# Where the spatial bias is added, when operands and weight sums are prepared, and which engine squares, in a three-stage kernel

## The chip, the cores and the metric

The program runs on one core of one Trainium2 chip. The metric is device microseconds of one execution, as the median of several runs. TensorE, VectorE, ScalarE, GpSimd and SyncE are called PE, DVE, ACT, POOL and SP, as in the profile; PEld is PE's weight load. SP and POOL issue the DMAs here: SP's queue takes nearly all loads, POOL's takes the stores, the scatters and the accumulating DMAs.

## The reference

Three parts follow one another on 4 batches of 3072 positions with 256 channels:

```python
scores = scale * np.matmul(z, z.transpose(0, 2, 1))
attn = np.maximum(scores, 0.0) ** 2
x = u * np.matmul(attn, v)                                   # attention
out[mask] = gate_w * eom * (relu(x[mask] @ w1[e]) @ w2[e])   # 8 experts, one for each token
u, v = split(relu(x @ w_in))                                 # 512 + 512 channels
v_n = (v - mean) / sqrt(var + 1e-6)
v_s = np.einsum('ts,bsd->btd', w_spatial, v_n) + b_spatial[None, :, None]
out = (u * v_s) @ w_out
```

The change concerns the bias `b_spatial` (one number for each position t), the operands of the einsum, and the squares of the attention.

## The kernel before

Every float32 operand is split into a rounded part `hi` (ACT copies it) and a remainder `lo` (DVE subtracts), and each product is three matmuls (hi by hi, lo by hi, hi by lo).

**Attention** (`attention`) makes 576 steps: 4 batches b, 6 column blocks j, 24 row blocks k. A step makes one 128x512 block of scores on PE, relu (ACT, `r`), the square rounded (ACT, `hi`), the square exact (`a`: ACT where `i % 3 == 1`, else DVE), the remainder (DVE, `lo`), and the product with v of three steps earlier. Beside it generators are pumped: `fore` (routing of the finished tokens, with indirect DMAs from POOL), `back` (loads and splits of the next batch; in the last batch, at j = 2, `w_prep` loads the first expert's weights through POOL's queue) and `slow`. From the second pass on, `slow` holds `first_sums`: 36 rounds, each with two loads of `w_spatial` into `raw4` buffers (three in all), four sums on DVE and four stores of the sums from POOL. A round takes five pumps. The buffers `raw4` serve `w_prep` too.

**Experts** (`moe`) and **produce** follow. `produce` makes u and v_n, writes u to `u_hid` and sums of v_n to `v_ops`.

**Products** (`products`) computes the einsum by a two-level scheme of seven products each (Strassen's in Winograd's form): seven outer products n in the order 1, 6, 7, 2, 5, 3, 4, and in each seven inner ones m in the order 1, 2, 6, 7, 5, 3, 4, each in two column halves tb, each in three steps kp. So there are 294 steps of 24 matmuls, and a group (n, m, tb) is three steps. Four of the outer products (2, 5, 3, 4, here called the finishing ones) give blocks of the output; the others are combined through a DRAM tensor `partial` with three slots X1, U2, U3: 1 writes X1, 6 reads X1 and writes U2, 7 reads U2 and writes U3, 2 reads X1, 5 reads U3 and adds to U2, 3 reads U2, 4 reads U3. Four things feed a step:

- `p_load` and `p_split`: the weights of a step come by SP into `raw` (three buffers, five steps ahead) and are split into `wh` (ACT, L1307) and `wl` (DVE, L1308) two steps ahead of their matmuls.
- `right`: 21 items (m, kk) for each n. It loads blocks of `v_ops` through SP into `ra` (and `rt` for m = 6, four blocks for an item), combines them on DVE (L1051 to L1059) and splits them (L1008 ACT, L1009 DVE). Each `yield` ends a pump; the queue `back` gets three pumps after each step.
- `evacuate`: after the last step of a group it combines the four PSUM banks with `ut` tiles (L1139 to L1149), and in four of the seven m adds the tile `xi` read from `partial` (two buffers; SP loads it in `x_load`, L1117). In a finishing product it then multiplies by `us` (u from `u_hid`, SP), splits the result into `gt` (L1181 ACT, L1184 DVE), and the gated tile goes to `out`, which multiplies by w_out and stores. In products 6 and 7 it stores `xi` to `partial` (L1168, POOL). `evacuate` advances by four pumps of `fore` after each step.
- The bias: it is added to slots of `partial` in DRAM by `add_bias`, an accumulating DMA from POOL that reads `b_spatial` for all 128 partitions and adds it to 768 KB: 8 of them to X1 during product 6, and 8 to U2 and 8 to U3 during product 7.

All engines but POOL run their instructions in the order in which the program issues them; POOL's order is shown below. A DMA whose source or buffer is not ready holds everything behind it in its queue.

Of the kernel before, what the change touches and what calls it, by code (L numbers as in the profile page):

```python
# [27 lines left out]
F32 = mybir.dt.float32  # L28
# [4 lines left out]
ALU = mybir.AluOpType  # L33
AX = mybir.AxisListType

P = 128
# [18 lines left out]
class _Kernel:  # L55
# [142 lines left out]
    def attention(self):  # L198
# [44 lines left out]
        for i, (b, j, k) in enumerate(steps):  # L243
# [25 lines left out]
            a = self.big.tile([P, 512], F32, name="a", bufs=2)  # L269
            if i % 3 == 1:  # L270
                nc.scalar.activation(a, r, AF.Square)  # L271
            else:
                nc.vector.tensor_tensor(a, r, r, op=ALU.mult)  # L273
# [11 lines left out]
            if i < NK:  # L285
                self.pump(self.back)
                self.pump(self.slow)
                self.pump(self.slow)
            elif i % 2 == 0 and (b == B - 1 or j in (1, 3, 4)):
                self.pump(self.slow)  # L290
# [722 lines left out]
    def right(self, n, dst):  # L1013
# [26 lines left out]
        for i, (m, kk) in enumerate(todo):  # L1040
            load(i + 1)
            yield
            if m == 7:
                a = t3.pop(kk)
            elif m == 4:
                a = t4.pop(kk)
            else:
                a = raws.pop(i)
# [33 lines left out]
    def products(self, steps, NR, pw, p_load, p_split, first):  # L1082
# [7 lines left out]
        block = lambda t: t.rearrange("p (d t) -> p d t", d=4)  # L1090
        ready, due, later, st, xin = deque(), deque(), deque(), {}, {}

        def at(m, tb):
            th, p = self.INNER[m]
            return p, (2 * th + tb) * 384
# [9 lines left out]

        def add(dst, src):
            nc.gpsimd.dma_start(dst, src, accum_op=ALU.add)

        def add_bias(src, m, tb, h):
            t = h * 1536 + at(m, tb)[1]  # L1110
            bias = self.bsp[t : t + 384].partition_broadcast(P).unsqueeze(1).to_broadcast([P, 4, 384])
            add(place(src, m, tb), bias)

        def x_load(n, m, tb):
# [4 lines left out]
        def u_load(n, m, tb, t):  # L1119
            b, t0 = target(n, m, tb)  # L1120
            nc.sync.dma_start(block(t), self.uh[b][:, :, t0 : t0 + 384])
            return t

        def evacuate(n, m, tb, acc):
# [6 lines left out]
            if m in (2, 5):  # L1131
                o = utile()
            us = None
            if o is not None and n in self.BLOCK:
                us = u_load(n, m, tb, self.ok.tile([P, 4 * 384], F32, name="us", bufs=1))
            for d in range(4):
# [21 lines left out]
            if n == 5:  # L1158
                add(place(self.U2, m, tb), block(o))
            r = xin.pop((m, tb))  # L1160
# [6 lines left out]
            if n not in self.BLOCK:  # L1167
                nc.gpsimd.dma_start(place(self.WRITES[n], m, tb), block(r))  # L1168
                if n == 6:
                    add_bias(self.X1, m, tb, 0)  # L1170
                else:
                    add_bias(self.U2, m, tb, 0)
                    later.append((self.U3, m, tb, 1))
                return
            for h in range(2):
                tt(wide(r, h), wide(r, h), wide(us, h), op=ALU.mult)
                yield
# [28 lines left out]
        for s, (n, m, tb, kp) in enumerate(steps[:-3]):  # L1206
# [17 lines left out]
            if kp == 2:  # L1224
                self.drain(self.fore)
                due.extend(ready)
                ready.clear()
                while later:
                    add_bias(*later.popleft())
                self.fore.append(evacuate(n, m, tb, acc))  # L1230
            for _ in range(4):
                self.pump(self.fore)
# [6 lines left out]
        x_load(n, m, tb)  # L1239
        us = u_load(n, m, tb, utile())  # L1240
        r, u, g = xin.pop((m, tb)), st["u", tb], []
# [19 lines left out]
        for h in range(2):  # L1261
            tt(wide(r, h), wide(r, h), wide(u, h), op=ALU.subtract)
        out(other[0], 0)
        column(1)
# [132 lines left out]
```

## Time and profile before

| | us |
|---|---|
| median of three runs | 3561.55 (3560.2 to 3566.04) |
| the profiled execution | 3547.28 |
| its span, first to last instruction | 3545.5 |
| PE busy | 3402.7 |
| DVE busy | 2535.8 |
| ACT busy | 1791.7 |
| POOL busy | 747.3 |

Busy time of the PE counts matmuls whatever clock they ran at, so a stretch in which the clock was down looks busier than what it achieved; the number of matmuls in a stretch tells more. The stages of the profiled execution are: attention to about 1130 us, experts to about 1760, produce to about 2070, products to the end.

### The profile page before, as it was taken

The numbers are of one execution on the slowest core, as the hardware profiler recorded it, in microseconds if no ns is written. First come the engines' busy times: TensorE is split into PE (matmuls) and PEld (weight loads), VectorE is DVE, ScalarE is ACT, GpSimd is POOL, SyncE is SP. The second block draws the span as 40 slices with busy tenths as digits, with TensorE's granted clock in tenths as the row PEclk, the third lists the DMA queues.
The fourth block names the chain that finished last, engine by engine and source line by source line (L and its number), as shares of the span: only waits on it lengthen the run. The fifth ranks groups of instructions, "written<-read, shape, count | busy, mean of one in ns | idle before, by whom it ended". The sixth has DMA issues, their size and how long they took to land.

```text
span 3545.5 us, 51148 instructions
## 1 busy us (share of the span) xinstructions
PE 3402.7 (96%) x18448; PEld 3094.1 (87%) x18448; DVE 2535.8 (72%) x4616; ACT 1791.7 (51%) x3110; POOL 747.3 (21%) x1092
## 2 busy tenths in 40 slices
PE   8999999999999999999999999996957999999999
PEld 6888887887787999999988889996957999999999
DVE  7777777788787788777588865664625776776766
ACT  8888878878776333333254533332312333343433
POOL 3111111121222566665423210000010000100000
PEclk9999999999999999999999999998978999999999
DMA  7232231233332777777477874979999577885754
GB/s 258 80 101 64 81 101 55 80 105 96 110 121 100 253 265 255 266 269 248 166 277 284 319 277 152 292 186 282 223 187 253 183 268 222 237 272 178 262 199 153
DMA packets 277480, 689.31 MB, mean 194 GB/s; under 512 B 30128, under 2 KB 126144, under 8 KB 277216
## 3 DMA queue, kind: packets, MB, share of 16 engines
q1 hardware_dynamic: 181536, 401.90, 33.9%
q0 software_dynamic: 95680, 284.06, 25.8%
q8 instruction: 145, 2.38, 0.3%
q14 instruction: 119, 0.97, 0.1%
HBM read 440.26 MB, written 264.45 MB: 199 GB/s over the span
## 4 chain that ended last, share of the span: by engine, by line
PE 72%; DMA 10%; issue 9%; POOL 3%; DVE 3%; ACT 2%; SPq 0%; POOLq 0%; DVEq 0%; ACTq 0%
PE bank L1195 10%; PE bank L1196 9%; PE bank L1194 9%; PE bank L226 7%; PE bank L227 7%; PE bank L225 7%; DMA ra<-v_ops 4%; PE bank L263 4%; PE bank L264 3%; PE bank L735 2%; PE bank L671 2%; PE bank L673 2%; PE bank L736 2%; PE bank L672 2%; PE bank L737 2%
## 5 line engine op out<-in xcount | busy, mean ns | idle before, releaser
L275 DVE TENSOR_TENSOR lo<-a,hi 128x512 fp32r<-128x512 f32 x576 | 398.2, 692 | 184.0 <-ACT a L271 93.9
L1194 PE MATMUL bank<-wh,R 128*128 128x384 f32 x1288 | 435.5, 338 | 49.1 <-ACT wh L1307 44.9
L1195 PE MATMUL bank<-wl,R 128*128 128x384 f32 x1288 | 436.2, 339 | 20.9 <-DVE wl L1308 20.9
L226 PE MATMUL bank<-lo,G 128*128 128x512 f32 x1152 | 451.9, 392 | 2.2 <-DVE lo L275 2.2
L225 PE MATMUL bank<-hi,G 128*128 128x512 f32 x1152 | 450.3, 391 | 0.0
L227 PE MATMUL bank<-hi,G 128*128 128x512 f32 x1152 | 449.7, 390 | 0.0
L1196 PE MATMUL bank<-wh,R 128*128 128x384 f32 x1288 | 434.9, 338 | 0.0
L1308 DVE TENSOR_TENSOR wl<-raw,wh 128x768 fp32r<-128x768 f32 x294 | 280.6, 955 | 197.2 <-ACT wh L1307 195.3
L266 ACT ACTIVATE r<-bank 128x512 f32<-128x512 f32 x576 | 342.5, 595 | 153.9 <-PE bank L264 144.2
L1307 ACT ACTIVATE wh<-raw 128x768 fp32r<-128x768 f32 x294 | 247.2, 841 | 337.7 <-PE bank L1196 193.9
L1194 PE MATMUL bank<-wh,K 128*128 128x384 f32 x1064 | 358.7, 337 | 19.2 <-ACT wh L1307 19.2
L1195 PE MATMUL bank<-wl,K 128*128 128x384 f32 x1064 | 359.1, 337 | 15.9 <-DVE wl L1308 15.9
L268 ACT ACTIVATE hi<-r 128x512 fp32r<-128x512 f32 x576 | 364.9, 633 | 18.3
L1196 PE MATMUL bank<-wh,K 128*128 128x384 f32 x1064 | 357.9, 336 | 0.0
L739 ACT ACTIVATE hh<-bank 128x512 fp32r<-128x512 f32 (+2 forms) x256 | 132.7, 518 | 392.2 <-PE bank L737 349.7
L1194 PEld LDWEIGHTS bank<-wh,R 128*128 128x128 f32 x1288 | 245.4, 191 | 51.7 <-ACT wh L1307 46.7
L273 DVE TENSOR_TENSOR a<-r 128x512 f32<-128x512 f32 x384 | 263.1, 685 | 23.9 <-ACT r L266 23.2
L1195 PEld LDWEIGHTS bank<-wl,R 128*128 128x128 f32 x1288 | 245.0, 190 | 24.2 <-DVE wl L1308 24.2
L226 PEld LDWEIGHTS bank<-lo,G 128*128 128x128 f32 x1152 | 217.1, 188 | 52.9 <-DVE lo L275 7.6
L225 PEld LDWEIGHTS bank<-hi,G 128*128 128x128 f32 x1152 | 217.2, 189 | 46.6 <-ACT hi L268 0.3
L741 DVE SCALAR_TENSOR_TENSOR hlo<-bank,hh 128x512 fp32r<-128x512 f32 (+2 forms) x256 | 150.6, 589 | 149.0 <-ACT hh L739 133.3
L227 PEld LDWEIGHTS bank<-hi,G 128*128 128x128 f32 x1152 | 217.1, 188 | 45.3
(298 smaller groups left out, 8048.9 us busy)
## 6 DMA issues: line engine op xcount, KB each, us to landing
raw<-w_parts SPq DMA_DIRECT2D x240, 384.0 KB
ra<-v_ops SPq DMA_DIRECT2D x147, 512.0 KB
raw<-wsq SPq DMA_DIRECT2D x126, 384.0 KB
v_ops<-vu POOLq DMA_DIRECT2D x84, 512.0 KB
xi<-partial SPq DMA_DIRECT2D x48, 768.0 KB
w_parts<-raw POOLq DMA_DIRECT2D x144, 192.0 KB
u_hid<-vu POOLq DMA_DIRECT2D x48, 512.0 KB
us<-u_hid SPq DMA_DIRECT2D x31, 768.0 KB
```

The costliest lines, as they stand in the source:

```text
L225: nc.tensor.matmul(acc[d], vh[:, c], hi, start=(k == 0), stop=False)
L226: nc.tensor.matmul(acc[d], vh[:, c], lo, start=False, stop=False)
L227: nc.tensor.matmul(acc[d], vl[:, c], hi, start=False, stop=(k == NK - 1))
L266: nc.scalar.activation(r, sb, AF.Relu, scale=1.0 / S)
L268: nc.scalar.activation(hi, r, AF.Square)
L273: nc.vector.tensor_tensor(a, r, r, op=ALU.mult)
L275: nc.vector.tensor_tensor(lo, a, _f(hi), op=ALU.subtract)
L1194: nc.tensor.matmul(ps, vh, wh[:, ws], start=(k == 0), stop=False)
L1195: nc.tensor.matmul(ps, vh, wl[:, ws], start=False, stop=False)
L1196: nc.tensor.matmul(ps, vl, wh[:, ws], start=False, stop=(k == 5))
L1307: nc.scalar.activation(hi, raw, AF.Copy)
L1308: tt(lo, raw, _f(hi), op=ALU.subtract)
```

## The change

Five things are changed. (1) The accumulating bias DMAs are gone. Each finishing product's `evacuate` loads 384 numbers of the bias for all partitions into a tile `bb` (192 KB, SP, right behind `us`) and adds it on DVE with two additions of 128x768, before the multiplication; the last group does the same. (2) `evacuate` is advanced by 3, 3 and 4 pumps in a group's steps instead of 4, 4, 4. (3) `right` yields once more in each item, and twice more at its first item of m = 6. (4) `first_sums` is pumped in other passes of the last batch: at every step of j = 1 and not at all in j = 2. (5) ACT makes a fourth of the squares `a` instead of a third.

```diff
-            if i % 3 == 1:
+            if i % 4 == 1:
                 nc.scalar.activation(a, r, AF.Square)
             else:
                 nc.vector.tensor_tensor(a, r, r, op=ALU.mult)
...
-            elif i % 2 == 0 and (b == B - 1 or j in (1, 3, 4)):
+            elif b == B - 1 and j == 1 or i % 2 == 0 and (j in (1, 3, 4) or b == B - 1 and j in (0, 5)):
                 self.pump(self.slow)
...
             load(i + 1)
             yield
+            yield
+            if m == 6 and kk == 0:
+                yield
+                yield
...
-        def add(dst, src):
-            nc.gpsimd.dma_start(dst, src, accum_op=ALU.add)
-
-        def add_bias(src, m, tb, h):
-            t = h * 1536 + at(m, tb)[1]
-            bias = self.bsp[t : t + 384].partition_broadcast(P).unsqueeze(1).to_broadcast([P, 4, 384])
-            add(place(src, m, tb), bias)
...
             nc.sync.dma_start(block(t), self.uh[b][:, :, t0 : t0 + 384])
-            return t
+            bb = self.ok.tile([P, 384], F32, name="bb", bufs=1)
+            nc.sync.dma_start(bb, self.bsp[t0 : t0 + 384].partition_broadcast(P))
+            return t, bb
...
             if n == 5:
-                add(place(self.U2, m, tb), block(o))
+                nc.gpsimd.dma_start(place(self.U2, m, tb), block(o), accum_op=ALU.add)
...
                 nc.gpsimd.dma_start(place(self.WRITES[n], m, tb), block(r))
-                if n == 6:
-                    add_bias(self.X1, m, tb, 0)
-                else:
-                    add_bias(self.U2, m, tb, 0)
-                    later.append((self.U3, m, tb, 1))
                 return
+            for h in range(2):
+                w = wide(r, h).rearrange("p (d t) -> p d t", d=2)
+                tt(w, w, bb.unsqueeze(1).to_broadcast([P, 2, 384]), op=ALU.add)
+                yield
...
-                while later:
-                    add_bias(*later.popleft())
                 self.fore.append(evacuate(n, m, tb, acc))
-            for _ in range(4):
+            for _ in range(4 if kp == 1 else 3):
                 self.pump(self.fore)
...
             tt(wide(r, h), wide(r, h), wide(u, h), op=ALU.subtract)
+            w = wide(r, h).rearrange("p (d t) -> p d t", d=2)
+            tt(w, w, bb.unsqueeze(1).to_broadcast([P, 2, 384]), op=ALU.add)
```

Lines behind the change have other numbers: L1308 is L1305 in the changed kernel, L1055 is L1059, L1168 is L1166, L1176 is L1173.

The first place is POOL's queue through products 7, 2 and 5. Before, the end of product 7 and the start of what follows (`bsp` is the bias, `xi` the tile that products 6 and 7 store, `os` an output block):

```order
L1107 DMA partial<-bsp 512x1x384 x2
L1168 DMA partial<-xi 512x1x384
L1107 DMA partial<-bsp 512x1x384 x2
L1168 DMA partial<-xi 512x1x384
L1107 DMA partial<-bsp 512x1x384 x2
L1168 DMA partial<-xi 512x1x384
L1107 DMA partial<-bsp 512x1x384
L1080 DMA out<-os 128x384 x16
L1107 DMA partial<-ut 512x1x384 x2
```

In the changed kernel, from product 1 to product 5:

```order
L1154 DMA partial<-ut 512x1x384 x8
L1166 DMA partial<-xi 512x1x384 x16
L1084 DMA out<-os 128x384 x16
L1157 DMA partial<-ut 512x1x384 x2
L1084 DMA out<-os 128x384 x4
```

The 24 accumulating DMAs that stood between the stores of `xi` are gone; the eight of `ut` in product 5 stay.

The second place is DVE at the start of the products. Before, from the last instruction of `produce`:

```order
L939 TENSOR_TENSOR vu_19995<-vu_19995,vu_19987 128x1024
L1308 TENSOR_TENSOR wl<-raw,wh 128x768
L1009 TENSOR_TENSOR K_74<-ra,K_74 128x512
L1009 TENSOR_TENSOR K_75<-ra,K_75 128x512
L1308 TENSOR_TENSOR wl<-raw,wh 128x768
L1009 TENSOR_TENSOR K_76<-ra,K_76 128x512
L1055 TENSOR_TENSOR rt<-rt,ra 128x1024
L1308 TENSOR_TENSOR wl<-raw,wh 128x768
```

In the changed kernel, from the second `wl` behind `produce`:

```order
L1305 TENSOR_TENSOR wl<-raw,wh 128x768
L1009 TENSOR_TENSOR K_81<-ra,K_81 128x512
L1009 TENSOR_TENSOR K_74<-ra,K_74 128x512
L1305 TENSOR_TENSOR wl<-raw,wh 128x768
L1009 TENSOR_TENSOR K_75<-ra,K_75 128x512
L1305 TENSOR_TENSOR wl<-raw,wh 128x768
L1009 TENSOR_TENSOR K_76<-ra,K_76 128x512
L1305 TENSOR_TENSOR wl<-raw,wh 128x768
L1059 TENSOR_TENSOR rt<-rt,ra 128x1024
L1305 TENSOR_TENSOR wl<-raw,wh 128x768
```

The first combination of m = 6 (`rt<-rt,ra`) stood behind two `wl` of the products stage and now stands behind five; in each of the seven products it has moved back by three.

The third place is DVE in a finishing product, a group of m = 3 in product 2. Before, from the evacuation of the banks to the gated tile:

```order
L1149 TENSOR_TENSOR ut<-bank_70,ut 128x384
L1149 TENSOR_TENSOR ut<-bank_71,ut 128x384
L1149 TENSOR_TENSOR ut<-bank_72,ut 128x384
L1149 TENSOR_TENSOR ut<-bank_73,ut 128x384
L1165 TENSOR_TENSOR xi<-xi,ut 128x768 x2
L1308 TENSOR_TENSOR wl<-raw,wh 128x768
L1176 TENSOR_TENSOR xi<-xi,us 128x768 x2
L1009 TENSOR_TENSOR K_77<-ra,K_77 128x512
L1308 TENSOR_TENSOR wl<-raw,wh 128x768
L1184 TENSOR_TENSOR gt<-xi,gt 128x768 x2
```

In the changed kernel, the same group up to the multiplication:

```order
L1147 TENSOR_TENSOR ut<-bank_70,ut 128x384
L1147 TENSOR_TENSOR ut<-bank_71,ut 128x384
L1147 TENSOR_TENSOR ut<-bank_72,ut 128x384
L1147 TENSOR_TENSOR ut<-bank_73,ut 128x384
L1163 TENSOR_TENSOR xi<-xi,ut 128x768
L1305 TENSOR_TENSOR wl<-raw,wh 128x768
L1163 TENSOR_TENSOR xi<-xi,ut 128x768
L1170 TENSOR_TENSOR xi<-xi,bb 128x768 x2
L1305 TENSOR_TENSOR wl<-raw,wh 128x768
L1173 TENSOR_TENSOR xi<-xi,us 128x768 x2
```

The bias stands where the multiplication stood, and the multiplication and all behind it come one `wl` later.

## Rows read from the trace of the kernel before

**Rows 1.** The page's chain that ended last: shares of the span by engine

```profile
PE 72%; DMA 10%; issue 9%; POOL 3%; DVE 3%; ACT 2%; SPq 0%; POOLq 0%; DVEq 0%; ACTq 0%
```

**Rows 2.** Stretches: start:end, length, busy us (instructions) by engine, PE clock, DMA share, GB/s

```profile
2060.00:2080.00 20.00, 12.15 (x67) 11.83 (x66) 7.24 (x10) 2.86 (x6) 1.25 (x2) 0.89 0.85 305
2080.00:2380.00 300.00, 300.00 (x1726) 300.00 (x1725) 195.14 (x274) 104.71 (x156) 12.83 (x15) 1.00 0.70 218
2380.00:2480.00 100.00, 71.61 (x367) 69.20 (x366) 47.53 (x61) 25.37 (x41) 8.54 (x9) 0.85 0.97 268
...
2580.00:2760.00 180.00, 116.26 (x599) 110.88 (x598) 75.84 (x101) 35.89 (x57) 15.55 (x15) 0.83 0.93 221
2760.00:3080.00 320.00, 320.00 (x1848) 320.00 (x1847) 225.53 (x310) 119.21 (x182) 20.54 (x30) 1.00 0.70 224
3080.00:3140.00 60.00, 55.74 (x311) 55.11 (x310) 39.94 (x52) 24.43 (x41) 6.31 (x9) 0.97 0.96 303
3140.00:3500.00 360.00, 360.00 (x2079) 360.00 (x2078) 255.86 (x348) 135.24 (x207) 13.56 (x25) 1.00 0.63 213
...
0.00:1140.00 1140.00, 1118.01 (x5026) 906.59 (x5027) 896.81 (x1884) 932.25 (x1637) 211.98 (x334) 1.00 0.31 104
```

**Rows 3.** The chain in 2550 to 2760 us: start, us, what

```profile
2560.33 14.73 DMA xi<-partial
...
2616.65 17.39 DMA partial<-xi
...
2636.39 17.49 DMA ra<-v_ops
```

**Rows 4.** The same chain by line, shares of its 210 us

```profile
by line: DMA ra<-v_ops 27.7%; DMA partial<-xi 14.7%; issue 11.5%; DMA xi<-partial 9.3%; PE bank L1195 8.8%; PE bank L1196 8.3%; PE bank L1194 8.0%; DVE wl L1308 3.2%; ACT wh L1307 2.0%; SPq L1025 1.4%; POOL partial L1107 1.1%; SPq L1300 1.0
```

**Rows 5.** SP's waits in 2550 to 2730 us: us in total, times, longest

```profile
SPq L1117 <- DMA partial<-xi: 53.5, 3, 23.6
```

**Rows 6.** DMA queues in 2440 to 2700 us: packets, MB, share of 16 engines

```profile
q0 software_dynamic: 9945, 18.94, 51.7%
q1 hardware_dynamic: 15217, 38.34, 41.7%
```

**Rows 7.** The bias DMAs on POOL: count, shortest/median/longest ns, first and last start

```profile
L1107 POOL DMA_DIRECT2D partial<-bsp x24: 1147/1166/1721, 2271.1 to 2707.9; - x24
```

**Rows 8.** DVE in order of time, finishing product 2: start, us, instruction, count [idle <-releaser]

```profile
2850.62 1.94 DVE L1149 TENSOR_TENSOR ut<-bank,ut 128x384 f32<-128x384 f32 x4
2852.48 1.81 DVE L1165 TENSOR_TENSOR xi<-xi,ut 128x768 f32<-128x768 f32 x2
2854.21 0.95 DVE L1308 TENSOR_TENSOR wl<-raw,wh 128x768 fp32r<-128x768 f32 x1
2857.63 1.82 DVE L1176 TENSOR_TENSOR xi<-xi,us 128x768 f32<-128x768 f32 x2 [2.47 <-DMA us<-u_hid]
...
2865.98 2.12 DVE L1149 TENSOR_TENSOR ut<-bank,ut 128x384 f32<-128x384 f32 x4 [0.38 <-PE bank L1196]
```

**Rows 9.** DVE in order of time at the start of the products

```profile
2076.37 1.23 DVE L1055 TENSOR_TENSOR rt<-rt,ra 128x1024 f32<-128x1024 f32 x1 [12.72 <-DMA ra<-v_ops]
2077.51 0.95 DVE L1308 TENSOR_TENSOR wl<-raw,wh 128x768 fp32r<-128x768 f32 x1
```

**Rows 10.** Attention: the stretch with the longest PE gap behind the start

```profile
960.00:980.00 20.00, 14.99 (x61) 11.81 (x60) 12.06 (x33) 11.10 (x23) 3.16 (x5) 0.83 0.31 103
```

**Rows 11.** Waits in 930 to 980 us: us in total, times, longest

```profile
ACT K L183 <- DMA raw<-w: 9.5, 3, 6.5
...
POOL raw L446 <- DMA w_parts<-raw: 4.2, 1, 4.2
```

**Rows 12.** Groups of instructions, the exact squares: busy us, mean ns | idle before

```profile
L273 DVE TENSOR_TENSOR a<-r 128x512 f32<-128x512 f32 x384 | 263.1, 685 | 23.9 <-ACT r L266 23.2
...
L271 ACT ACTIVATE a<-r 128x512 f32<-128x512 f32 x192 | 118.3, 616 | 0.6 <-DVE lo L275 0.6
```

**Rows 13.** Waits over the whole run: the multiplication by u

```profile
DVE xi L1176 <- DMA us<-u_hid: 27.1, 20, 3.2
```

**Rows 14.** DVE in order of time near the end: the second last group's gated tile

```profile
3519.56 1.83 DVE L1184 TENSOR_TENSOR gt<-xi,gt 128x768 fp32r<-128x768 f32 x2
```

More of the change, by code (lines that the diff above doesn't have):

```diff
@@ L1090, in products @@
         block = lambda t: t.rearrange("p (d t) -> p d t", d=4)
-        ready, due, later, st, xin = deque(), deque(), deque(), {}, {}
+        ready, due, st, xin = deque(), deque(), {}, {}
         def at(m, tb):
@@ L1134, in evacuate @@
             if o is not None and n in self.BLOCK:
-                us = u_load(n, m, tb, self.ok.tile([P, 4 * 384], F32, name="us", bufs=1))
+                us, bb = u_load(n, m, tb, self.ok.tile([P, 4 * 384], F32, name="us", bufs=1))
             for d in range(4):
@@ L1239, in products @@
         x_load(n, m, tb)
-        us = u_load(n, m, tb, utile())
+        us, bb = u_load(n, m, tb, utile())
         r, u, g = xin.pop((m, tb)), st["u", tb], []
```

## The prediction

> **What bounds the kernel now.** Read the chain that ended last first: PE holds 72% of it, DMA 10%, DVE 3%, ACT 2% [rows 1]. So the time is PE's work plus places where PE waits, and the waits at the end of which something else than PE comes last are mostly transfers. Next read the stretches [rows 2]. Where PE never stops, in 2760 to 3080 and in 3140 to 3500 us, it does 1848 matmuls in 320 us and 2079 in 360, both 5.775 a us. Measured with that rate, the other stretches of the products lost: 2380 to 2480, 577.5 wanted, 367 done, **36.5 us**; 2580 to 2760, 1039.5 wanted, 599 done, **76.3 us** (more than the 63.7 us in which PE is not busy, since the granted clock was 0.83 to 0.85 there, between the two levels of 1.2 and 2.4 GHz); 3080 to 3140, 346.5 wanted, 311 done, 6.1 us. The stretch 2060 to 2080 mixes two kinds of matmuls; by its busy time it lost 7.9 us. In attention 5026 matmuls in 1140 us are 4.41 a us, and 960 to 980 has 61 of 88 [rows 10], 6.2 us. These five sum to 133 us, and the first two are products 6 and 7, into whose time all the bias DMAs fall: 24 of them, from 2271 to 2708 us [rows 7].
>
> Then ask what PE waits for in the two large holes. In 2550 to 2760 the chain has pieces of xi being loaded, 9.3% of 210 us, of xi being stored, 14.7%, and of operands `ra` arriving, 27.7% [rows 3, 4]. SP waited 53.5 us in three pieces for stores of xi [rows 5]: the load of a further xi needs a buffer that POOL's queue has yet to empty, and in that queue a bias DMA stands ahead of each store. All loads of weights and operands stand behind SP's wait. Meanwhile the transfer engines are full, 0.93 to 0.97, at only 221 to 268 GB/s, while product 2 moves 224 GB/s at a share of 0.70 [rows 2]; POOL's queue took 51.7% of the engines' time for 18.94 MB, SP's 41.7% for 38.34 [rows 6]. A byte of the former cost 2.5 times as much.
>
> **1. The bias DMAs go.** 24 transfers of 768 KB leave, and with them the wait of each store of xi behind one. What remains in products 6 and 7 is loads of weights, operands and xi, and 16 stores, much as in product 2, which replaces the stores by loads of u and runs with PE full [rows 2]. A store of xi then still takes somewhere between the time of its bytes at 224 GB/s, 786 KB, 3.5 us, and the 17.39 us of the jam [rows 3]; I take 6, near the lower end, as nothing stands before it. The load that needs the buffer comes some 12 us (three steps of 24 matmuls) behind the group's end, the store about 6 behind it, so at 6 us nothing waits, and at 17 us SP waits some 11, which five steps of prefetch nearly cover. A burst of operand loads may still delay weights at the end of each product, as in 3080 to 3140 [rows 2], where accumulating DMAs of another kind run. So of 113 us I take 105 as won, with bounds 50 (if the pieces of `ra`, half of the chain's transfer time in the hole [rows 4], stay) and 113.
>
> A check by bytes, without waits: 24 times 786 KB are 18.9 MB, at the 221 GB/s of the hole [rows 2] 85 us. By the Trainium skill, "DMA: Bandwidth & Descriptors", section "Issuing engines are not separate DMA queues", transfers that different engines issue run on the same 16 engines and interleave, so that only the transfers themselves count and not that they stood in POOL's queue. By that page the win would be nearer to the 85, and the forecast 20 us higher; the trace speaks for a dearer byte on that queue [rows 6], and I keep 105.
>
> **2. `right` yields more.** The first combination of m = 6 waits 12.72 us for its load, and the `wl` that PE needs stands right behind it on DVE [rows 9]. It now stands three `wl` later, that is three steps of 24 matmuls, 12.5 us: the wait is almost exactly covered. Of the 7.9 us I take 7 (0 to 8). The same move helps in 3080 to 3140: 3 of 6.1 (0 to 6). Twenty-three more yields make 99 pumps an outer product where 126 are given, so the operands come in time; if not, PE would wait for a split. What is behind a moved item on SP, the loads of `raw`, gets ahead of its four loads, which is the better order.
>
> **3. Sums of `first_sums`.** The stall at 960 is w_prep and the sums sharing three buffers: ACT waits 9.5 us for expert weights, POOL 4.2 for a store of sums before it can load them [rows 11]. With no sums in j = 2 that wait goes: 6 us (0 to 6). j = 1 of the last batch gets 12 more pumps, 4.8 rounds of four sums, about 10 us of DVE in 46; DVE has 897 of 1140 busy in this stage [rows 2], so it fits, at a cost of 0 to 4 us, taken as 1. Behind a late sum on DVE stand the remainders `lo`, which PE wants three steps later.
>
> **4. Squares.** 48 squares leave ACT, 48 x 0.616 = 30 us, and 48 x 0.685 = 33 us come to DVE [rows 12]. ACT was at 82% of the stage and DVE at 79% [rows 2]; they change places, PE keeps its work, and I take 0 (-2 to +3). PE's matmuls are the cover; without it the worst is 33 us.
>
> **5. The bias on DVE.** A 128x768 addition starts 0.87 us before the next one (2852.48 to 2854.21 for two, [rows 8]). There are 64 of them, 55 us. In a finishing group DVE's work is 1.86 for the banks and nine operations of 0.87, 9.7 us, and becomes 11.4; with four splits of `right` some 14; PE's group is 96 matmuls, 16.6 us. It fits. What is delayed: the gated tile comes one `wl` later, and `out`, the next group's evacuation and the splits of weights stand behind it. The bias may wait for its load, which SP issues behind that of u; u itself was waited for in 20 places, 27.1 us in all, 3.2 at the most [rows 13]. In place of that wait the later multiplication has none. I take 0.2 us for each of 31 groups, 6 us (0 to 30).
>
> **6. The end.** The gated tile of the second last group is made by DVE at 3519.56 to 3521.4, just as PE wants it [rows 14]. Two additions stand before it now: 2 us (0 to 4).
>
> Sum: 105 + 7 + 3 + 6 - 1 - 6 - 2 = **112 us** against the profiled execution's 3547.3, which gives 3435. The median of the runs is 14.3 us above that execution; whether those 14 us are part of the holes the trace can't show. I let them stand and predict **3449**.
>
> **Rivals.**
> - *Half of the holes stays.* For it: the pieces of `ra` are the largest part of the chain there [rows 4], and the burst hurts at 3080 too, with no bias. Against it: the full stretches have the same bursts. Only 50 of 113 are won: 3504.
> - *DVE becomes the bound.* By the Trainium skill, "Perfetto Trace Analysis", section "Optimizing Scalar/DVE Operations", work should leave the Vector engine when that is the saturated one; this change brings it 88 us. In this kernel that would be DVE chains of finishing groups longer than PE's 16.6 us, so that all 55 us lie on the path instead of 6: 3498. The trace speaks against it: 9.7 us of work [rows 8].
> - *The load of the bias is late* (slower). It stands behind 768 KB of u on SP. A group has 16.6 - 14 = 2.6 us of room on DVE, and 112 us in 31 groups are 3.6 more: from some 6.2 us of waiting in each group the gain is eaten. At 10 us, the kernel is at 3561 + 31 x 3.8, about 3680. The longest wait for u was 3.2 [rows 13].
> - *It does not do what it says:* the holes come from the traffic of products 6 and 7 alone, and removing the bias only moves the wait. Then steps 2 and 3 balance 5 and 6, and the time is about 3555.
>
> **How the numbers follow.** The forecast has 0.70, half of the holes 0.14, DVE 0.08, no effect 0.05, the late load 0.03. The forecast's own bounds: all 113 us won, all of steps 2 and 3, nothing lost and the 14 us gone as well, 3412; 85 won and 20 lost on DVE, 3483. The first two rivals end at 3504; with some DVE loss beside them, 3512. So the range is **3408 to 3512**. A measurement of this kernel can tell about 0.2%, 7 us, from no change. Faster: 0.70 + 0.14 + 0.08 and half of the fourth, 0.94; same 0.02; slower 0.04.
>
> **What would show it.** In the new profile products 6 and 7 should take as many us a matmul as product 2, with the clock at 1.00 and no wait of SP for stores of xi over a few us; the transfer share there should fall from 0.95 to about 0.8. The m = 6 combination at the start should wait little, and no PE gap should stand at 2070 or 960. DVE should be busy in 2760 to the end for some 8 points more, and PE still full. Wrong would be: holes of tens of us in products 6 and 7 with `ra` at the end of the wait; waits of the bias addition of over 3 us in most groups; or PE waiting for `wl` in finishing groups.

## The result and the profile after

| | median of the runs | lowest to highest | profiled execution | its span |
|---|---|---|---|---|
| before | 3561.45 us (4 runs) | 3560.20 to 3566.04 | 3547.28 us | 3545.5 us |
| after | 3418.72 us (4 runs) | 3417.67 to 3421.45 | 3417.67 us | 3415.8 us |

The changed kernel takes 0.9598 of the time before, 95% interval 0.9582 to 0.9615: 143 us by the medians, 129.7 us by the two profiled spans. Of what is forecast above, 3449 us in 3408 to 3512, the time came out 30 us lower.

The first and the fourth part of the page after: busy time, share of the span and instructions by engine, and the chain that ended last.

```profile
PE 3377.8 (99%) x18448; PEld 3080.5 (90%) x18448; DVE 2622.0 (77%) x4728; ACT 1774.9 (52%) x3062; POOL 717.5 (21%) x1068
...
PE 46%; DVE 1%; issue 0%; DMA 0%; ACT 0%; SPq 0%; ACTq 0%; DVEq 0%
```

DMA held 10% of the chain before [rows 1] and now 0%; the chain after can be followed back to some 1758 us only, which is why its shares sum to 47%, but it takes in all the products. PE is the bound nearly everywhere there. The stretches after answer to [rows 2] and [rows 10]. The columns are the same: start:end, length, busy us (instructions) of PE, PEld, DVE, ACT and POOL, PE's clock, DMA share, GB/s. The products begin some 11 us earlier now, so 2240 to 2720 holds nearly all of products 6 and 7 in both kernels, and after the start of product 2 as well.

```profile
0.00:1140.00 1140.00, 1122.94 (x5063) 912.71 (x5063) 933.42 (x1939) 911.85 (x1594) 211.96 (x335) 1.00 0.32 105
...
960.00:980.00 20.00, 20.00 (x94) 16.35 (x93) 17.57 (x48) 16.43 (x30) 3.24 (x4) 0.99 0.18 55
...
2060.00:2080.00 20.00, 20.00 (x117) 20.00 (x117) 14.43 (x16) 9.26 (x15) 0.00 (x0) 1.00 1.01 380
...
2240.00:2640.00 400.00, 397.98 (x2297) 397.69 (x2296) 284.26 (x390) 145.20 (x215) 12.51 (x18) 1.00 0.72 245
2640.00:2720.00 80.00, 80.00 (x463) 80.00 (x462) 58.07 (x84) 29.77 (x44) 2.17 (x4) 1.00 0.59 192
2720.00:3380.00 660.00, 654.39 (x3762) 652.95 (x3761) 507.61 (x677) 248.83 (x383) 37.70 (x59) 1.00 0.73 238
```

Read each against 5.775 matmuls a us. 2240 to 2640 wants 2310 and did 2297: 2.3 us lost. 2640 to 2720 wants 462 and did 463: nothing. For the kernel before, the same two stretches are:

```profile
2240.00:2640.00 400.00, 347.10 (x1935) 343.07 (x1934) 224.96 (x311) 112.42 (x168) 33.89 (x34) 0.94 0.89 231
2640.00:2720.00 80.00, 42.25 (x199) 39.88 (x200) 29.24 (x39) 16.18 (x27) 7.37 (x7) 0.73 1.01 243
```

There it lost 64.9 and 45.5 us. So 108 of 110 us of the holes are gone. The start gap is gone too. 2720 to 3380, the finishing products, wants 3811.5 and did 3762: 8.6 us lost, the most that is left. In attention 5063 matmuls stand where 5026 stood [rows 2], 37 more; at 4.41 a us that is 8.4 us.

What waits after, in 2060 to 3380 us (for whom and for what: us in total, times, longest). All of PE's waits:

```profile
PE bank L1073 <- DVE ut L1139: 4.6, 3, 2.4
PE bank L1073 <- ACT R L1008: 2.0, 1, 2.0
PE bank L1073 <- DVE ut L1147: 1.0, 1, 1.0
```

Of the waits for a transfer, those of DVE and of ACT in the same stretch, and one of SP's over the whole run:

```profile
DVE xi L1170 <- DMA bb<-bsp: 17.5, 14, 2.5
...
ACT R L1008 <- DMA ra<-v_ops: 8.2, 6, 3.2
ACT K L1008 <- DMA ra<-v_ops: 7.1, 5, 2.3
...
SPq L1113 <- DMA partial<-xi: 7.3, 4, 2.3
```

SP waits 7.3 us for stores of xi in the whole run, where one stretch alone had 53.5 [rows 5]. The first combination of m = 6 waits 2.78 us at the start, where it waited 12.72 [rows 9]. The bias is waited for 14 times, 2.5 us at the most.

### The profile page after: what moved, and what is told of

Same layout as the page of the kernel before. It is cut to its first block, busy times and chain, and to the rows that moved or that the text cites. A ratio compares the mean times of both kernels' runs of the same rounds, so it can differ in the third digit from the quotient of the medians.

```text
span 3415.8 us, 51212 instructions
## 1 busy us (share of the span) xinstructions
PE 3377.8 (99%) x18448; PEld 3080.5 (90%) x18448; DVE 2622.0 (77%) x4728; ACT 1774.9 (52%) x3062; POOL 717.5 (21%) x1068
## 5 line engine op out<-in xcount | busy, mean ns | idle before, releaser
L1305 DVE TENSOR_TENSOR wl<-raw,wh 128x768 fp32r<-128x768 f32 x294 | 280.9, 955 | 212.3 <-ACT wh L1304 211.2
L1191 PE MATMUL bank<-wh,R 128*128 128x384 f32 x1288 | 430.4, 334 | 0.0
L1193 PE MATMUL bank<-wh,R 128*128 128x384 f32 x1288 | 430.2, 334 | 0.0
L273 DVE TENSOR_TENSOR a<-r 128x512 f32<-128x512 f32 x432 | 296.4, 686 | 26.5 <-ACT r L266 26.0
```

The costliest lines, as they stand in the source:

```text
L1191: nc.tensor.matmul(ps, vh, wh[:, ws], start=(k == 0), stop=False)
L1193: nc.tensor.matmul(ps, vl, wh[:, ws], start=False, stop=(k == 5))
L1305: tt(lo, raw, _f(hi), op=ALU.subtract)
```

## The experiments

All ratios are against the kernel before, run on the same chip as the kernel in question; there its median was 3549.6 to 3553.2 us. "Lost" is counted as above, with 5.775 matmuls a us. A few windows lie some us apart between kernels.

### What the bias transfers cost, and of what kind the cost is

**e1_bias_dve**: before with part 1 alone.

```diff
...
-                if n == 6:
-                    add_bias(self.X1, m, tb, 0)
-                else:
-                    add_bias(self.U2, m, tb, 0)
-                    later.append((self.U3, m, tb, 1))
...
+            bb = self.ok.tile([P, 384], F32, name="bb", bufs=1)
+            nc.sync.dma_start(bb, self.bsp[t0 : t0 + 384].partition_broadcast(P))
...
+            for h in range(2):
+                w = wide(r, h).rearrange("p (d t) -> p d t", d=2)
+                tt(w, w, bb.unsqueeze(1).to_broadcast([P, 2, 384]), op=ALU.add)
+                yield
...
```

> The kernel before with the first edit alone: no accumulating bias DMAs, the bias loaded into bb and added by DVE in the finishing products; pumps of evacuate, right, sums and squares as before. Theory Q (the holes of products 6 and 7 come from the bias DMAs): most of the 143 us that the changed kernel gained is here, a median of about 3450 us, and products 6 and 7 without PE gaps over some us. Theory R (the bursts of operand loads carry half of the holes): about 3500.

Measured: 3467.18 us, ratio 0.977 (0.9754 to 0.9787). That lies between the two theories' times. The holes themselves are gone, as the first says: 2281 and 463 matmuls in 2240 to 2640 and 2640 to 2720 us, 5.0 us lost of 110. What is missing to 3450 us is lost in the finishing products, as the next run shows.

**e7_no_bias**: before without the bias transfers and without any addition.

```diff
                 nc.gpsimd.dma_start(place(self.WRITES[n], m, tb), block(r))
-                if n == 6:
-                    add_bias(self.X1, m, tb, 0)
-                else:
-                    add_bias(self.U2, m, tb, 0)
-                    later.append((self.U3, m, tb, 1))
```

> The kernel before without the bias DMAs and with no addition in their place: the bias is left out of the result. Beside e1 it tells what the 64 additions on DVE and the 32 small loads cost. Prediction's sum: 6 us less than e1, with bounds 0 and 30. If DVE is the bound of the finishing products: 30 to 55 us less than e1.

Measured: 3439.78 us, ratio 0.9692 (0.9676 to 0.9708). The transfers cost 3.1%, 109 us. But the additions on DVE, with their loads, cost 27 of these in the order of before, as e1 is that much slower; the forecast of 6 is missed and lies within its bounds of 0 and 30. The finishing products show where. First e7, with the larger part of products 6 and 7, then e1:

```profile
2240.00:2640.00 400.00, 397.14 (x2285) 395.54 (x2285) 278.25 (x381) 142.85 (x218) 11.39 (x16) 1.00 0.73 252
...
2720.00:3380.00 660.00, 655.44 (x3769) 654.41 (x3768) 469.31 (x635) 250.41 (x387) 37.60 (x59) 1.00 0.70 231
```

```profile
2060.00:2080.00 20.00, 12.12 (x61) 11.80 (x61) 7.21 (x9) 4.65 (x9) 0.00 (x0) 0.78 0.84 311
...
2720.00:3380.00 660.00, 641.49 (x3633) 637.30 (x3632) 490.35 (x658) 244.84 (x379) 36.00 (x56) 0.98 0.71 229
```

In the last of these stretches e7 lost 7.4 us, e1 30.9. The start gap (61 matmuls of 115) is in both.

**e8_bias_aside**: before, with the same 24 accumulating transfers into rows of `y_tok` that the products don't read.

```diff
...
-            add(place(src, m, tb), bias)
+            i = self.aside % 16
+            self.aside += 1
+            dst = self.yt[i * 768 : (i + 1) * 768, :].rearrange("(p r) d -> p (r d)", p=P)
+            nc.gpsimd.dma_start(dst.rearrange("p (a t) -> p a t", a=4), bias, accum_op=ALU.add)
```

> The kernel before with the same 24 accumulating bias DMAs, at the same places of POOL's queue and with the same bytes, but added to rows of a DRAM tensor that nothing reads any more (y_tok), so that no load or store of partial depends on them; the bias is left out of the result. Theory W (waiting: loads of xi hold SP's queue because of the order between bias, stores and loads on partial): the holes go almost as in e7, within 30 us of it. Theory T (the transfer engines' time is what is short): the holes stay, 80 us or more above e7, though SP's wait for stores of xi is shorter.

Measured: 3552.35 us, ratio 1.0005 (0.9995 to 1.0014). It did not tell the two theories apart as meant. POOL issued the transfers earlier, from 1793 to 2134 us, in the stage `produce`. That stage still loads from `y_tok` (until 2098 us), so the rows are not free there: on POOL the transfers wait 23.3 us for those loads and 59.6 us for one another, and the stores of `v_ops`, which the products read, stand behind them in the queue. The last of these stores comes at 2173.8 us, where before has it at 2060.4, 113 us later. The hole moved with them:

```profile
2060.00:2200.00 140.00, 87.16 (x391) 73.05 (x390) 73.42 (x141) 40.23 (x77) 29.76 (x42) 0.80 0.97 283
```

The transfer engines are full here too, and products 6 and 7 were full of matmuls (2295 and 447). What it does show: the same transfers cost the same at another place, with no load of xi behind them. Other stores stood behind them there, so it doesn't separate the engines' time from the waits.

**e10_copy_plain** and **e11_copy_accum**: e7 with 24 transfers of 768 KB pinned behind the stores of products 6 and 7. They take the result just stored as their source and write rows that nobody reads. e11 accumulates; e10 has the same lines without `accum_op`.

```diff
...
                 nc.gpsimd.dma_start(place(self.WRITES[n], m, tb), block(r))
+                for _ in range(1 if n == 6 else 2):
+                    i = self.aside % 16
+                    self.aside += 1
+                    dst = self.yt[i * 768 : (i + 1) * 768, :].rearrange("(p r) d -> p (r d)", p=P)
+                    nc.gpsimd.dma_start(dst.rearrange("p (a t) -> p a t", a=4), place(self.WRITES[n], m, tb), accum_op=ALU.add)
```

> Built on the kernel without bias (e7_no_bias: before without the 24 bias transfers and without an addition, 3439.8 us, 0.969 of before; the bias is left out of the output). Behind each store of the subtree products, where the bias transfers stood on GpSimd's queue, it puts a plain copy of 768 KB from the partial result just stored to a buffer that nobody reads any more: 24 copies, one behind each store of product 6 and two behind each of product 7, no accumulation. Theory (an accumulating transfer holds the DMA engines for about 7.4 us, a plain one of the same bytes for 2 to 4.5 us, and this engine time is the damage): the copies add at most 24 x 4.5 = 108 us of engine time to a stretch that has slack for about that, so 3440 to 3475 us, 0.969 to 0.978 of before. Rival (the damage comes of the place in the queue: the store is written, its slot is read back and written again before the next load may follow, whatever the kind): 3510 to 3560 us, 0.99 to 1.0, like e11_copy_accum.

> The same kernel as e10_copy_plain with the one difference that the 24 copies accumulate into the buffer that nobody reads (bias left out of the output). Theory (engine time of accumulating transfers): about 177 us of all DMA engines in products 6 and 7 again, as in the kernel before, so most of the 110 us that leaving the transfers out gave is lost again: 3510 to 3560 us, 0.99 to 1.0 of before, and the software queue's share between 2260 and 2720 us is near 46%. Rival (the reader's wait for the accumulated slot was what cost, not engine time): nobody reads these rows, so 3440 to 3480 us, and alike with e10_copy_plain.

Measured: e10 3451.69 us, 0.9714 (0.9698 to 0.973); e11 3480.86 us, 0.9798 (0.9782 to 0.9814). By the ratios plain copies cost 0.22% over e7, 8 us, with an error about as large, as e7 ran on another chip; by the matmuls below, 16 us. Either is inside the theory's 0 to 35, and the rival falls: the place in the queue alone does not cost 70 us or more. Accumulating copies cost 1.06% over e7, 38 us, and 29 us more than the plain ones, on the same chip. So neither expectation for e11 holds: the kind matters, against the rival, but less than the theory said (3510 us or more; POOL's queue should have held near 46% of the engines' time in 2260 to 2720 us, and held 31.4%). Products 6 and 7 in e10, then in e11:

```profile
2240.00:2640.00 400.00, 387.46 (x2197) 383.24 (x2195) 262.90 (x359) 133.37 (x204) 27.66 (x41) 0.99 0.81 290
2640.00:2720.00 80.00, 79.43 (x456) 78.65 (x456) 57.19 (x80) 30.99 (x47) 2.19 (x4) 1.00 0.59 200
```

```profile
2240.00:2640.00 400.00, 374.44 (x2094) 370.43 (x2094) 250.06 (x344) 127.19 (x192) 35.58 (x38) 0.97 0.86 265
2640.00:2720.00 80.00, 73.64 (x404) 72.16 (x403) 53.00 (x69) 27.49 (x45) 4.35 (x6) 0.96 0.82 261
```

Lost: 20.6 us in e10, 47.4 in e11, 110.4 in before, and 4.3 in e7. SP's waits for the stores of xi grow with them. In 2060 to 2720 us, e10, e11 and before have the following, and e7 has no such wait:

```profile
SPq L1118 <- DMA partial<-xi: 4.1, 2, 3.0
```

```profile
SPq L1118 <- DMA partial<-xi: 33.7, 6, 13.1
```

```profile
SPq L1117 <- DMA partial<-xi: 85.2, 5, 23.6
```

In e10 and e11 no load of xi reads what the 24 transfers write. So the longer waits of e11 come from transfers before the stores in POOL's queue, or from the engines that these hold, and not from slots that are read again. The price of one transfer can be read from POOL's queue on the pages (packets, MB, share of 16 engines over the span). In order: e7, e10, e11, e8, before.

```profile
q0 software_dynamic: 83008, 265.18, 21.6%
```

```profile
q0 software_dynamic: 87616, 284.06, 22.9%
```

```profile
q0 software_dynamic: 95680, 284.06, 24.3%
```

```profile
q0 software_dynamic: 95680, 284.06, 25.2%
```

```profile
q0 software_dynamic: 95680, 284.06, 25.8%
```

Times their spans (3434.3, 3453.6, 3478.2, 3551.8, 3545.5 us) and less e7's 741.8 us, the 24 transfers of the same 18.9 MB held all 16 engines for 49, 103, 153 and 173 us: **2.0 us** for a plain copy, **4.3** for an accumulating one, **6.4 and 7.2** for an accumulating one whose source is the broadcast bias (384 numbers read 512 times). A plain copy is 192 packets, an accumulating one 528. So accumulating adds 2.3 us, and the repeated source 2.1 to 2.9 more.

The packets in the traces say where the last part comes from. Of the 528 packets 512 carry 1536 bytes. These take 140 ns in the median in e11, in e8 and in before alike, but 143, 213 and 237 ns in the mean: 2% of them take over 160 ns in e11, 28% in e8 and 31% in before. The slow ones come with the repeated source, at both of its places; the eight accumulating transfers of product 5, whose source is a tile, have a mean of 143 ns as well (e7). Summed by packets the prices come out a little higher, 4.6, 6.8 and 7.6 us, as the queue's other packets took a little less than in e7.

The waits of xi's loads for these very slots, which e11 has not, were not separated from the source: from e11 to before the time rises by some 70 us, and the engines' time by 70 as well.

### What the yields of `right` do

**e2_right_late**: before with part 3 alone.

```diff
             load(i + 1)
             yield
+            yield
+            if m == 6 and kk == 0:
+                yield
+                yield
```

> The kernel before with the added yields of right alone; the bias DMAs stay. Theory Q: only the gap at the start of the products (8 us) and part of that at 3080 us go, the two large holes stay: about 3550. Theory R: the loads of operands are what ends the waits, so spreading them takes half of the holes away: about 3500.

Measured: 3514.6 us, ratio 0.9896 (0.988 to 0.9913): 35 us by the medians and 37 by the ratio, for three added yields. That lies between the two theories' times.

```profile
2060.00:2080.00 20.00, 20.00 (x117) 20.00 (x116) 12.19 (x15) 9.59 (x17) 0.00 (x0) 1.00 1.01 372
...
2240.00:2640.00 400.00, 340.87 (x1893) 335.54 (x1891) 220.22 (x306) 108.70 (x162) 34.29 (x34) 0.93 0.91 232
2640.00:2720.00 80.00, 61.66 (x291) 58.60 (x292) 41.35 (x55) 23.63 (x38) 6.24 (x6) 0.83 1.02 269
2720.00:3380.00 660.00, 659.98 (x3808) 659.66 (x3807) 478.03 (x641) 257.26 (x397) 37.59 (x59) 1.00 0.72 234
```

The start is full, the finishing products lost 0.6 us (9.6 in before), and the holes stay, some 9 us smaller (2184 matmuls in the two stretches, where before had 2134). So spreading the operands' loads does not close the holes, and the yields gain at places that neither theory named.

**e5_undo_right**: the changed kernel without part 3.

```diff
-            yield
-            if m == 6 and kk == 0:
-                yield
-                yield
```

> The changed kernel without the added yields of right. If the yields only matter beside the bias DMAs (e2 alone gave 35 us), this stays within 15 us of the changed kernel: about 0.964 of before. If the finishing products need them too, because DVE's additions stand before loads of operands that come late, as e1 (27 us above e7) lets one think, it falls back by 30 us or more: about 0.970 or above.

Measured: 3460.48 us, ratio 0.9741 (0.9727 to 0.9756), so the yields are worth 1.4%, 51 us, in the changed kernel: the second of the two expectations. Two of its stretches, and two waits in 2060 to 3380 us, PE's first and ACT's for `ra`:

```profile
2060.00:2080.00 20.00, 12.77 (x58) 12.45 (x58) 12.37 (x13) 6.56 (x12) 0.00 (x0) 0.74 0.91 343
...
2720.00:3380.00 660.00, 632.32 (x3574) 625.44 (x3573) 482.58 (x645) 238.57 (x370) 36.07 (x56) 0.99 0.70 228
```

```profile
PE bank L1187 <- ACT os L1079: 20.9, 9, 3.4
...
ACT R L1008 <- DMA ra<-v_ops: 67.6, 12, 13.1
...
ACT K L1008 <- DMA ra<-v_ops: 48.6, 13, 10.3
```

It lost 41.1 us in the finishing products and 10 at the start. ACT waited 116 us for pieces of `ra`; after, 15.3. One such wait, first SP and then ACT in order of time (start, us, instruction, count, [idle <-releaser]):

```profile
2973.91 0.52 SPq L1113 DMA_DIRECT2D us<-u_hid  x1
2974.49 0.61 SPq L1115 DMA_DIRECT2D bb<-bsp  x1
2975.28 0.52 SPq L1109 DMA_DIRECT2D xi<-partial  x1
2978.87 0.33 SPq L1293 DMA_DIRECT2D raw<-w_parts  x1
2979.24 1.50 SPq L1025 DMA_DIRECT2D ra<-v_ops  x2
```

```profile
2974.86 0.85 ACT L1300 ACTIVATE wh<-raw 128x768 fp32r<-128x768 f32 x1 [2.34 <-issue]
2988.51 0.63 ACT L1008 ACTIVATE R<-ra 128x512 fp32r<-128x512 f32 x1 [12.81 <-DMA ra<-v_ops]
2989.05 0.48 ACT L1079 ACTIVATE os<-bank 128x384 f32<-128x384 f32 x1
2989.42 0.84 ACT L1300 ACTIVATE wh<-raw 128x768 fp32r<-128x768 f32 x1
```

SP issues `us`, `bb`, `xi` and `raw` ahead of the two pieces of `ra`. ACT reaches the copy of `ra` at 2975.7 and stands there until 2988.5. Behind it, in ACT's own order, stand `os`, which empties PE's banks, and `wh`, of which DVE makes the next `wl`. PE stops soon after:

```profile
2995.33 0.44 PE L1187 MATMUL bank<-wh,K 128*128 128x384 f32 x1 [3.39 <-ACT os L1079]
```

**e13_one_yield**: the changed kernel without the two extra yields at m = 6.

```diff
-            if m == 6 and kk == 0:
-                yield
-                yield
```

> The changed kernel without the two extra yields before the first combination of m = 6; the one more yield before every combination stays. Without any of the new yields the changed kernel takes 3460.5 us (0.974), with all 0.960. Theory (the one yield in every step does it: it lengthens the way from each load to the copy on ScalarE that waits for it, and ScalarE's evacuations stand behind that copy): 3415 to 3430 us, 0.960 to 0.964. Rival (it is the first combination of m = 6 alone, four tiles at once, that is late): 3445 to 3465 us, 0.970 to 0.976.

Measured: 3413.93 us, ratio 0.9608 (0.9592 to 0.9624), as the changed kernel. The one yield for each item does the work. The rival falls.

The waits of ACT for `ra` and the loss go together over the runs, though not in one ratio. In 2720 to 3380 us the waits are 76.9 us in e1, 63.4 in e5, 31.9 in e7, 7.1 in e2 and 3.4 in e12 (below); lost are 30.9, 41.1, 7.4, 0.6 and 0.8 us. That the wait on ACT is what stops PE is seen in the chain above; no run changed it alone.

### DVE's additions in the changed order

**e12_after_no_bias**: the changed kernel without loads of the bias and additions; the yields of the pumps stay.

```diff
...
-            for h in range(2):
-                w = wide(r, h).rearrange("p (d t) -> p d t", d=2)
-                tt(w, w, bb.unsqueeze(1).to_broadcast([P, 2, 384]), op=ALU.add)
-                yield
+            yield
+            yield
...
```

> The changed kernel without the bias (neither its loads nor VectorE's additions; the pumps' yields stay, so the order of the rest stays), bias left out of the output. In the order of before, without the yields in the right operands' combinations, the additions and loads cost 27 us (3467.2 with, 3439.8 without). Theory (the additions cost only where ScalarE and VectorE already stand behind a late right operand, and the yields have taken that away): 3405 to 3420 us, 0.957 to 0.961, 0 to 10 us under the changed kernel. Rival (VectorE's time itself costs, 62 additions of 0.95 us and the loads of 24 more transfers): 3385 to 3400 us, 0.951 to 0.955, 20 to 30 us under the changed kernel.

Measured: 3406.35 us, ratio 0.9586 (0.957 to 0.9602); its span is 3408.8 us, 7.0 under that of after.

```profile
2720.00:3380.00 660.00, 659.87 (x3807) 659.55 (x3806) 466.14 (x632) 254.85 (x387) 38.14 (x60) 1.00 0.71 232
```

It lost 0.8 us in the finishing products, after 8.6. So the additions and loads that cost 27 us in e1 cost about 7 here (4 by the ratios, which can't tell it from nothing), and the theory holds.

One more rival is a late bias: in e1 the additions wait for `bb`, and in after less. The waits of DVE in 2060 to 3380 us in e1, then in e6, the changed kernel without part 2 (next section):

```profile
DVE xi L1166 <- DMA bb<-bsp: 64.5, 24, 4.6
```

```profile
DVE xi L1170 <- DMA bb<-bsp: 51.0, 23, 4.3
```

e6 still waits 51.0 us where e1 waits 64.5, and yet it is as fast as the changed kernel; in 2720 to 3380 us it did 3782 matmuls and lost 5.1 us. In the products the two differ by the yields of `right` alone. So the late bias is not what cost 27 us in e1.

### The small parts

**e3_sums_moved**, **e4_squares**: before with part 4 alone, and with part 5 alone. **e6_four_pumps**: the changed kernel without part 2.

```diff
-            elif i % 2 == 0 and (b == B - 1 or j in (1, 3, 4)):
+            elif b == B - 1 and j == 1 or i % 2 == 0 and (j in (1, 3, 4) or b == B - 1 and j in (0, 5)):
...
-            if i % 3 == 1:
+            if i % 4 == 1:
...
-            for _ in range(4 if kp == 1 else 3):
+            for _ in range(4):
```

> The kernel before with the fourth edit alone (first_sums pumped at every step of j = 1 and not in j = 2 of the last batch). Prediction: the PE gap near 960 us (6 us) goes, 0 to 4 us are lost in j = 1: 5 us less than before, 0.15%. Rival: a round of sums stays in flight through j = 2 and holds two of the three raw4 buffers, so that w_prep waits in another place: same within 2 us.

> The kernel before with the fifth edit alone (a fourth of the exact squares on ACT). Prediction: 0, within -3 and +2 us of before. Rival (DVE or ACT bounds attention): 30 us more, or up to 30 us less.

> The changed kernel with four pumps of evacuate after each step instead of 3, 3 and 4. If the slower pumping carries part of the gain (the additions are spread and wl comes earlier on DVE), it is 10 to 25 us slower than the changed kernel: about 0.964 to 0.967 of before. If not, within 5 us: 0.960.

Measured: e3 3549.75 us, 0.999 (0.9979 to 1.0); e4 3549.0, 0.999 (0.9982 to 0.9999); e6 3410.2, 0.9604 (0.9589 to 0.9618). None can be told from its neighbour by time alone. In attention, 0 to 1140 us, e3 did 5045 matmuls and e4 5044, 19 and 18 more than the 5026 of before, 4.3 and 4.1 us, and together the 8.4 of the changed kernel. The same code did 5025 to 5035 there in before, e1, e2, e7, e8, e10 and e11, so each of these figures is uncertain by some 2 us.

## Why the prediction was right, and where it was not

The spans split as follows: before to e7, 111.2 us gained; e7 to e12 (parts 2 to 5 in a kernel without bias), 25.5; e12 to after (the bias comes back on DVE), 7.0 lost. That is the 129.7 us.

- **Step 1, 105 us:** 111.2 in the spans, 109 by the ratio. The size was right, and so was the wait: the stores of xi stood behind these transfers, and SP's loads behind the stores. What it left open is why the wait was long: the transfer holds the sixteen engines for 7.2 us in before, where a plain copy takes 2.0. Of the 109 us, some 8 to 16 are what plain copies cost at this place, and 29 are shown to come from accumulating (e10 to e11); some 70 more come with the repeated source and the dependence of xi's loads on the slots. The packets speak for the source, but no run parts the two. The check by bytes gave 85 us, since it priced all bytes alike. The page named there, "DMA: Bandwidth & Descriptors" of the Trainium skill, also says in "Rules for kernel authors" that an accumulate reads its destination and writes it later; it gives no price. The queue's packets and time agree with more work per byte: 528 packets where a copy has 192, and 4.3 us where it has 2.0. That transfers of different engines share the same sixteen agrees with the hole of before, where the two queues' shares sum to 93% [rows 6].
- **Step 2, 10 us:** this is the term that was mis-sized: 35 to 37 us alone (e2), 51 in the changed kernel (e5), and still some 17 in a kernel without any bias (e7 to e12, 25.5 less attention's 8.4). The sum took only the two gaps seen in the trace before, 7.9 and 6.1 us. It looked at DVE's first combination at m = 6 alone, where the start gap is (8.7 us gained in e2); e13 shows that the two extra yields there matter little. The wait that the traces point to is ACT's, at the copies of pieces of `ra`, with evacuations and `wh` behind it; before, these waits were 68.7 and 62.0 us in 2060 to 3360 us (31 of them in the finishing products, most of the rest in the holes), and no step of the sum asked whose work stood behind them:

```profile
ACT R L1008 <- DMA ra<-v_ops: 68.7, 16, 15.9
...
ACT K L1008 <- DMA ra<-v_ops: 62.0, 12, 31.0
```

- **Step 5, 6 us lost:** 7.0 in the changed kernel, by e12. It was right only because step 2 was in the same change, which is luck as far as the sum goes: in the order of before the additions cost 27 us (e1 against e7), near the upper bound of 30, and the yields take that away (e1 against e6). That late operands had used up the groups' room is the likely reading, not shown by a run of its own. The two terms could not be added one by one. The Trainium skill's page "Perfetto Trace Analysis", "Optimizing Scalar/DVE Operations", adds a case for engines that aren't saturated but cause bubbles on others; the trace of e5 agrees, ACT being busy 239 of 660 us there while PE waits for its evacuations. What that section advises for the case, breaking up instructions, no run here tried.
- **Step 3, 5 us:** 4.3 by the matmuls of e3, which is right within the 2 us of doubt; by time it can't be told from nothing. The gap at 960 is gone, but 920 to 960 has a smaller hole of its own now: 166 matmuls in e3 and 160 after, where before has 181. That is the expectation's rival in part. Twelve more pumps are 2.4 rounds, not 4.8.
- **Step 4, 0 us:** 4.1 gained by the matmuls of e4, 2.4 by the medians; the bound was a gain of 3, and the doubt is 2.
- **Step 6, 2 us lost:** not seen apart from the rest.
- **The 14.3 us** that were let stand were not there after: the median is 1.05 us above the profiled execution. In the experiments, on other chips, before's median was 3549.6 to 3553.2 us, near the profiled execution. Yet the ratios agree (e6 0.9604, after 0.9598), so the chip of the main comparison may have been slower for both kernels. What the 14 us were, no run showed.

The sum of the forecast on the profiled execution, 3435, lay 17 us above the 3417.67 measured: counted in the order e7, e12, after, step 1 gave 6 more than said, steps 3 and 4 together 3, step 2 with the end some 9, and step 5 cost 1 more. These differences mix chips and are each uncertain by several us. The 14 us come on top for the median. Of its bounds, the lower one adds up to 3414 by the terms named, not 3412. Of the rivals, "half of the holes stays" falls by 2.3 us left of 110, "DVE becomes the bound" by e12, the late load by 2.5 us at most and by e6, and "does not do what it says" by e7. Of the signs, the transfer share in products 6 and 7 fell further than said, to 0.72; DVE rose from 71% to 77% of 2720 to 3380 us, 6 points where 8 were said.

## What to carry to other kernels

A queue's time over the span, divided by its transfers, tells what one kind of transfer costs the sixteen engines; compare kinds by that and not by bytes, and take a small addend that is read many times to an engine that handles the data anyway. Where an in-order engine makes a copy that waits for a load, list what stands behind it in its own order before pricing the wait by the gap it now shows. Terms that use the same slack (late operands and added work in a finishing group) can't be priced one by one: undo each from the changed kernel as well as doing each alone.

## What was not expected of the hardware

Transfers of the same 768 KB differ 3.6 times in what they hold of the engines: 2.0 us for a copy within device memory, 4.3 accumulating, 6.4 to 7.2 accumulating from a repeated 1.5 KB source, where some 30% of the packets are slow. And POOL issued transfers that no later part reads some 480 to 570 us earlier than the same transfers in before (e8), so that such an experiment has to tie them to a place, as e10 and e11 do.
